# Decay attention and two gated MLPs on one core: table transfers, first weight loads, pair order of the second layer, and where each down projection begins

## The chip, the cores and the metric

The kernel runs on one core of one Trainium2 chip. The metric is the device time of one execution in microseconds (us); the lower the better. Three runs of the kernel before gave a median of 528.17 us (527.85 to 528.56).

## What is computed

Three stages follow one another, all in float32 precision (sizes: 2 batches, 8 heads, 768 positions, 64 wide; 1536 tokens of 512).

```python
# attention with decay, blocks of 64 in the reference (128 in the kernel)
out[b] = (q_b k_b^T * Dmask) v_b + (q_b * lam^(i+1)) state
state  = lam^block * state + (k_b * lam^(block-1-i))^T v_b
x = out as 1536 x 512
# first MLP
x = ((x @ w_a) * (x @ w_b)) @ w_out          # inner width 1536
# second MLP
x = max(x @ w1, x @ w2, x @ w3) @ w_out2      # inner width 768
```

## The kernel before, in words

**Precision.** TensorE multiplies float32 values as two parts each, hi and lo, and three products (hi hi, hi lo, lo hi) are added in PSUM. Every operand is therefore split first: ScalarE (ACT) copies it to hi, and VectorE (DVE) or GpSimd (POOL) subtracts to get lo. The weights come as 8-byte numbers and are converted on the core before that: one raw tile `wr` of 1 MB (768 KB for a piece of a down projection) is turned into float32 by DVE (L223, L228, L236) and ACT (L226, L232, L234). The weight tiles are numbered in one list: 0 to 11 first layer up, 12 to 19 first layer down, 20 to 28 second layer up, 29 to 32 second layer down.

**Attention.** There are 12 steps n (6 chunks of 128 positions, 2 batches). Step n needs `aq` (queries and keys) and `av` (keys and values), 512 KB each, and two decay tables made on the core: `powers` computes a row of powers per head, stores it to DRAM (`tab_d`), and `tables` (L352) and `decay_rows` (L357) read it back into the tile `tables`, in four transfers of 128 KB (the mask `dmask`) and four of 64 KB (`ltab`). In the loop over n, step n issues the loads of `aq` n+4 and `av` n+3, then the scores of n+2 (`s`, L397), their masking on DVE (`am`, L420), and the output of step n: products with the values (`o`, L436), with the state (L441), and the state's update (L448), which DVE reads (`stt`, L460, L462). The raw weight tile 0 is loaded and its conversion opened at n = 2, tile 1 at n = 7. From n = 7 on a group of plain first-layer products (`p`, L555) is put behind each step.

**Layers up.** Past the first two weight tiles of layer one, a weight tile is multiplied by one of two halves j of the tokens in seven products of a Strassen scheme (six matmuls each; L537). A tile and both halves are called a pair here. The products of neighbouring groups are interleaved by the table `SLOT`. Three PSUM banks belong to a group: `z`, `b` and `x`. Products 1, 6, 7 and 4 add into `z` one after another, and ACT copies the bank after 1, 6 and 7 (`z1`, `z6`, `z7`), so each of these copies stands between two products. In layer two the operands of half j are `y0...` and `y1...`: A11, A12, A22 and four sums S1 to S4, made by DVE and ACT from the output of the first layer down. `plan2` orders the first two pairs of layer two as (0,0), (1,0), (0,1), (1,1): tile 0 and 1 with half 0, then both with half 1.

**Layers down.** `down1` (L668) runs over k = 0 to 11 and three thirds t of the tokens: first t = 0 and 1 together, then t = 2 (`yp`, L654, 12 matmuls for each (t, k)). `down2` (L703) makes the output tiles (`out`, L700).

**What sets the order.** All queues are written by the program in one order: the class `Pace` keeps an estimate of each engine's time and puts DVE, ACT and POOL work into the stream when its gate is open. Gates are opened by hand, by `open_to("conv", item)` and `open_to("split", item)`, at points that follow TensorE's work. Each engine then works strictly in its order. All transfers of interest are issued by SyncE (SP), in one queue. Pools: 26 slots of 6 KB per partition, 5 buffers `hp` for weights and their hi and lo, 2 raw tiles, 8 PSUM banks.

Of the kernel before, what the change touches and what calls it, by code (L numbers as in the profile page):

```python
# [16 lines left out]
C = 128  # L17
# [145 lines left out]
def decay_attention_gated_mlps(ctx: ExitStack, tc: tile.TileContext, qkv: bass.AP, lam: bass.AP, wup: bass.AP, wdown: bass.AP, out: bass.AP):  # L163
# [115 lines left out]
    def down_block(m, i):  # L279
        roomy = 2 <= i < ND1 or i == ND1 + 3  # L280
# [19 lines left out]
    def items_to(m):  # L300
        while state["item"] <= min(m, len(items) - 1):
            n = state["item"]
            kind, i = items[n]
            wtask[n] = pace.opens["done", n] = pace.add((up_pair if kind == "up" else down_block)(n, i), {0: -1, 2: 0.5}.get(n, 1))
            state["item"] += 1
# [46 lines left out]
    def tables():  # L352
        for g in range(2):
            for odd in range(2):
                nc.sync.dma_start(out=dmask[:, g, odd:NP:2], in_=view((2 * odd + (g ^ odd)) * 2 * C, [[1, 128], [8 * C, NP // 2], [1, C]]))

    def decay_rows():  # L357
        for hh in range(2):
            for odd in range(2):
                nc.sync.dma_start(out=ltab[64 * hh:64 * hh + 64, odd:NP:2], in_=view((2 * odd + (hh ^ odd)) * 2 * C + C, [[0, 64], [8 * C, NP // 2], [1, C]]))  # L360
# [307 lines left out]
    def down1(at):  # L668

        ps = [[bank(f"yp{t}{e}") for e in range(KD)] for t in range(2)]  # L670
        for k in range(K1):
            for t in range(2):
                at(t, k)
                down1_part(t, k, ps[t])
        ps = [bank(f"yp2{e}") for e in range(KD)]
        for k in range(K1):
            at(2, k)
            down1_part(2, k, ps)
# [24 lines left out]
    def down2():  # L703

        n = NT // 128
        ps = [bank(f"out{i}") for i in range(6)]
        for k in range(K2):
            for i in range(6):
                down2_part(i, k, ps[i], slice(0, 512))
                if k == K2 - 1:  # L710
                    store(i, 0, 512, ps[i])
        for i in range(6, n):
            last = i == n - 1
            cols = 256 if last else 512
            for c in range(0, 512, cols):
                p = bank(f"out{i}_{c}")[:, c:c + cols]
                for k in range(K2):
                    down2_part(i, k, p, slice(c, c + cols))
                store(i, c, cols, p, last and c > 0)

    with tc.manual_schedule():
# [35 lines left out]
        def finished1(at, g):  # L757

            if g.j == 1:
# [4 lines left out]
                if m + 2 < N1:  # L764
                    open_to("split", m + 2)
                if m == K1 - 2:
# [3 lines left out]
                if m == K1 - 1:  # L770
                    for d in range(4, ND1):
# [15 lines left out]
        def layer1_steps():  # L787
# [9 lines left out]
            yield from in_slots([Group(f"u{i}_{j}", i, j, xo.get, gated) for i, j in plan], each1, finished1)  # L797

        layer1 = layer1_steps()
        for n in range(len(order)):  # L800
            load(n + 4, 0)
            load(n + 3, 1)
            if n in (2, 7):
                m = n // 4
                load_to(m)
                open_to("conv", m)
                open_to("split", m)
# [22 lines left out]
        def at1(t, k):  # L830
            if (t, k) == (2, 0):
                yo[0] = Operands([ya[0, b] for b in range(B)], "y0")
            if t == 2:
                pace.open(("y0", k - 3))
            if (t, k) == (2, 4):
                open_to("split", base + 1)
                open_to("conv", base + 2)

        down1(at1)
# [6 lines left out]
        def finished2(at, g):  # L846
            n = g.n - N1
            f, i = divmod(n, 3)
            if g.j == 1:
# [5 lines left out]
                for d in {N2 - 2: (0, 1), N2 - 1: (2, 3)}.get(n, ()):  # L855
# [15 lines left out]
        plan2 = [(0, 0), (1, 0), (0, 1), (1, 1)] + [(n, j) for n in range(2, N2) for j in range(2)]  # L871
        groups = [Group(f"v{n}{j}", N1 + n, j, yo.get, largest(n // 3, n % 3)) for n, j in plan2]
        for _ in in_slots(groups, each2, finished2):
            pass
        down2()
# [63 lines left out]
```

## Time and profile before

| what | value |
|---|---|
| median of 3 runs | 528.17 us |
| the profiled execution's own time | 528.49 us |
| its span, first to last instruction | 526.7 us |
| TensorE (PE) busy | 508.4 us, 97% |
| DVE, ACT, POOL busy | 364.1, 284.8, 50.5 us |
| PE busy in 10:50 us | 32.17 of 40 us |
| PE busy in 50:92 us | 42.00 of 42 us |
| PE busy in 230:240 us (end of layer one up) | 9.42 of 10 us |
| PE busy in 337:400 us (start of layer two up) | 60.01 of 63 us |
| PE busy in 465:480 us (end of layer two up) | 13.73 of 15 us |
| PE busy in 500:527 us (last products, last store) | 23.68 of 27 us |

Busy time is the time in which an engine has an instruction in work. A busy PE is not a PE at full clock: the table of stretches gives the granted clock too. Stretches that are not listed are without idle time on PE. Engines in the profile: PE matmul, PEld weight load, DVE VectorE, ACT ScalarE, POOL GpSimd, SP SyncE (SPq its queue).

### The profile page before, as it was taken

The page shows a single profiled execution, that of the slowest core. Times are in us where ns is not written, and L with a number is a line of the kernel's source. Part 1 is how long each engine was busy: PE and PEld are TensorE (multiplying, and loading weights), DVE is VectorE, ACT ScalarE, POOL GpSimd, SP SyncE. Part 2 cuts the span into 40 slices and gives each one's busy share as a digit, 9 for nine tenths or more (in the row PEclk, how much of TensorE's full clock was granted, in tenths as well). Part 3 has the DMA queues.
Part 4 walks back from the last instruction along what each step waited for, and adds up shares of the span by engine and source line. Part 5 has one row for each costly group of instructions (what it writes and reads, how often), then busy time and mean ns, then how long its engine had stood idle before and what let it go on. Part 6 is the DMA issues. An engine that isn't in the chain of part 4 may idle for free.

```text
span 526.7 us, 7797 instructions
## 1 busy us (share of the span) xinstructions
PE 508.4 (97%) x3175; PEld 469.2 (89%) x3175; DVE 364.1 (69%) x546; ACT 284.8 (54%) x451; POOL 50.5 (10%) x46
## 2 busy tenths in 40 slices
PE   6879999999999999999999999998999999999997
PEld 3757899999999999998888888798999999988886
DVE  3267878886677766679969268385899998689000
ACT  1257754665545555367868366445476557366211
POOL 1673000011111111111000000000000000000000
PEclk9979999999999999999999999999999999999999
DMA  7995310222222111113542200100222211020221
GB/s 225 401 403 192 103 60 0 81 80 81 80 81 82 80 44 24 54 62 120 180 160 80 81 0 22 59 1 0 81 80 82 81 60 59 2 88 33 98 83 61
DMA packets 11812, 47.96 MB, mean 91 GB/s; under 512 B 1272, under 2 KB 3072, under 8 KB 9088
## 3 DMA queue, kind: packets, MB, share of 16 engines
q1 hardware_dynamic: 11776, 47.46, 25.1%
q8 instruction: 25, 0.41, 0.3%
q14 instruction: 11, 0.09, 0.1%
HBM read 44.30 MB, written 3.15 MB: 90 GB/s over the span
## 4 chain that ended last, share of the span: by engine, by line
PE 86%; DVE 5%; DMA 4%; ACT 2%; issue 1%; SPq 1%; ACTq 0%; DVEq 0%
PE yp L654 19%; PE zu L537 16%; PE zv L537 13%; PE out L700 9%; PE bu L537 8%; PE p L555 7%; PE bv L537 7%; PE xu L537 4%; PE xv L537 3%; DMA wr<-wup_dram 2%; DMA aq<-qkv_dram 1%; PE o L436 1%; DVE m L597 1%; ACT stt L466 1%; DVE lo L187 1%
## 5 line engine op out<-in xcount | busy, mean ns | idle before, releaser
L187 DVE TENSOR_TENSOR lo<-w,hi 128x1024 fp32r<-128x1024 f32 (+1 forms) x40 | 44.1, 1109 | 11.8 <-ACT hi L190 11.8
L190 ACT ACTIVATE hi<-w 128x1024 fp32r<-128x1024 f32 (+1 forms) x40 | 37.1, 952 | 12.8 <-DVE w L187 10.1
L654 PE MATMUL yp<-gh,dh 128*128 128x512 f32 x108 | 42.0, 389 | 0.0
L654 PE MATMUL yp<-gl,dh 128*128 128x512 f32 x108 | 42.0, 389 | 0.0
L654 PE MATMUL yp<-gh,dl 128*128 128x512 f32 x108 | 42.0, 389 | 0.0
L586 POOL TENSOR_TENSOR g<-z1u,z6u 128x384 f32<-128x384 f32 x20 | 25.1, 1258 | 172.8 <-DVE z6u L568 155.4
L236 DVE TENSOR_TENSOR w<-w,ws 128x1024 f32<-128x1024 f32 x21 | 26.5, 1262 | 16.0 <-ACT w L234 15.9
L187 DVE TENSOR_TENSOR gl<-g,gh 128x512 fp32r<-128x512 f32 x36 | 25.8, 725 | 13.3 <-ACT gh L190 13.3
L228 DVE SCALAR_TENSOR_TENSOR w<-wr,w 128x1024 int32<-128x1024 int32 (+1 forms) x26 | 31.0, 1193 | 0.2
L234 ACT ACTIVATE w<-w 128x1024 f32<-128x1024 f32 (+1 forms) x26 | 26.3, 1012 | 7.4 <-DVE w L228 7.2
L226 ACT ACTIVATE ws<-wr,bias 128x1024 f32<-128x1024 f32 x21 | 25.8, 1228 | 7.6 <-DMA wr<-wup_dram 7.6
L187 DVE TENSOR_TENSOR w<-w 128x256 f32<-128x256 f32 (+1 forms) x57 | 29.0, 509 | 0.8
L190 ACT ACTIVATE z7u<-zu 128x384 f32<-128x384 f32 x20 | 9.8, 491 | 35.5 <-PE zu L537 35.4
L689 DVE COPY ob<-out 128x256 f32<-128x256 f32 x1 | 0.4, 425 | 36.9 <-PE out L700 36.9
L654 PEld LDWEIGHTS yp<-gh,dl 128*128 128x128 f32 x108 | 20.3, 188 | 4.2
L654 PEld LDWEIGHTS yp<-gl,dh 128*128 128x128 f32 x108 | 20.3, 188 | 4.2
L232 ACT ACTIVATE ws<-ws,bias 128x1024 f32<-128x1024 f32 x21 | 24.0, 1144 | 0.0
L654 PEld LDWEIGHTS yp<-gh,dh 128*128 128x128 f32 x108 | 20.3, 188 | 4.1
L223 DVE TENSOR_SCALAR w<-wr 128x1024 int32<-128x1024 int32 (+1 forms) x26 | 17.5, 674 | 8.7 <-DMA wr<-wup_dram 8.6
L190 ACT ACTIVATE ob<-out 128x512 f32<-128x512 f32 (+1 forms) x12 | 7.0, 580 | 29.2 <-PE out L700 28.8
L568 DVE TENSOR_TENSOR z7u<-bu,z7u 128x384 f32<-128x384 f32 x20 | 11.1, 556 | 15.4 <-ACT z7u L190 15.4
L190 ACT ACTIVATE gh<-g 128x512 fp32r<-128x512 f32 x36 | 21.5, 618 | 0.0
(200 smaller groups left out, 1495.2 us busy)
## 6 DMA issues: line engine op xcount, KB each, us to landing
wr<-wup_dram SPq DMA_DIRECT2D x21, 1024.0 KB, 4.8
wr<-wdown_dram SPq DMA_DIRECT2D x12, 768.0 KB, 4.3
aq<-qkv_dram SPq DMA_DIRECT2D x12, 512.0 KB, 7.3
av<-qkv_dram SPq DMA_DIRECT2D x10, 512.0 KB, 9.6
out_dram<-ob SPq DMA_DIRECT2D x11, 256.0 KB, 2.0
tables<-tab_d SPq DMA_DIRECT2D x4, 128.0 KB, 3.7
av<-qkv_dram SPq DMA_DIRECT2D x2, 256.0 KB, 4.8
tables<-tab_d SPq DMA_DIRECT2D x4, 64.0 KB, 4.1
```

The costliest lines, as they stand in the source:

```text
L187: (nc.vector if e == "DVE" else nc.gpsimd).tensor_tensor(out=o, in0=a, in1=b, op=op)
L190: nc.scalar.activation(out=o, in_=a, func=AF.Copy)
L226: nc.scalar.activation(out=sign, in_=high.bitcast(F32), func=AF.Identity, bias=bias[:, 0:1])
L228: nc.vector.scalar_tensor_tensor(out=w, in0=low, scalar=29, in1=w, op0=ALU.logical_shift_right, op1=ALU.bitwise_or)
L232: nc.scalar.activation(out=sign, in_=sign, func=AF.Sign, bias=bias[:, 1:2])
L234: nc.scalar.activation(out=f, in_=f, func=AF.Abs)
L236: nc.vector.tensor_tensor(out=f, in0=f, in1=sign, op=ALU.mult)
L537: nc.tensor.matmul(ps, w, x, start=p in FIRST and i == 0, stop=i == len(todo) - 1, skip_group_check=p not in FIRST)
L555: nc.tensor.matmul(ps, w[:, 128 * k:128 * k + 128], x[:, k], start=m == 0, stop=m == 11)
L586: nc.gpsimd.tensor_tensor(out=ga[g.n][:, tokens(g.j, 0)], in0=g.z[1], in1=g.z[6], op=ALU.mult)
L654: nc.tensor.matmul(ps[e], w[:, cols], g, start=k == 0 and m == 0, stop=k == K1 - 1 and m == 2)
L700: nc.tensor.matmul(ps, a[:, o:o + 128], w[:, s], start=k == 0 and n == 0, stop=k == K2 - 1 and n == 2)
```

## The change

- The masks come by one transfer and the decay rows by two, since the heads are now ordered on the host in the way that the tile wants them.
- Raw weight tile 0 is loaded at n = 0 and tile 1 at n = 3 (before: 2 and 7); their conversion opens at n = 3 and 6 (before: 2 and 7).
- `plan2` takes layer two pair by pair: (0,0), (0,1), (1,0), (1,1).
- `down1` and `down2` become generators. The first piece of `down1`, (t, k) = (0, 0), is issued before the last two products of layer one up; the first two pieces of `down2` (output tiles 0 and 1, k = 0) before the last two products of layer two up, one ahead of each.
- Conversions of down tiles 12, 13 and 29, 30 open a pair or so earlier; those of 18 and 19 later, inside `down1`. Down tile 13 moves to a slot, 19 to an `hp` buffer.

```diff
--- before.py
+++ after.py
@@ -277,7 +277,7 @@
     dparts, dunit = {}, {}
 
     def down_block(m, i):
-        roomy = 2 <= i < ND1 or i == ND1 + 3
+        roomy = 1 <= i < ND1 - 1 or i == ND1 + 3
         yield "gate", ("done", m - (2 if roomy or i == ND1 + 1 else 1))
         yield "gate", ("conv", m)
         t = yield from converted(m, WB, roomy)
@@ -301,7 +301,7 @@
         while state["item"] <= min(m, len(items) - 1):
             n = state["item"]
             kind, i = items[n]
-            wtask[n] = pace.opens["done", n] = pace.add((up_pair if kind == "up" else down_block)(n, i), {0: -1, 2: 0.5}.get(n, 1))
+            wtask[n] = pace.opens["done", n] = pace.add((up_pair if kind == "up" else down_block)(n, i), {0: -1, 2: 0.5, 3: 0.6}.get(n, 1))
             state["item"] += 1
 
     def open_to(what, m):
@@ -350,14 +350,11 @@
         return bass.AP(tensor=a.tensor, offset=a.offset + offset, ap=ap)
 
     def tables():
-        for g in range(2):
-            for odd in range(2):
-                nc.sync.dma_start(out=dmask[:, g, odd:NP:2], in_=view((2 * odd + (g ^ odd)) * 2 * C, [[1, 128], [8 * C, NP // 2], [1, C]]))
+        nc.sync.dma_start(out=dmask.rearrange("p g a i -> p (g a) i"), in_=view(0, [[1, 128], [2 * C, H], [1, C]]))
 
     def decay_rows():
         for hh in range(2):
-            for odd in range(2):
-                nc.sync.dma_start(out=ltab[64 * hh:64 * hh + 64, odd:NP:2], in_=view((2 * odd + (hh ^ odd)) * 2 * C + C, [[0, 64], [8 * C, NP // 2], [1, C]]))
+            nc.sync.dma_start(out=ltab[64 * hh:64 * hh + 64], in_=view(hh * NP * 2 * C + C, [[0, 64], [2 * C, NP], [1, C]]))
 
 
     order = [(b, c) for c in range(NC) for b in range(B)]
@@ -667,11 +664,14 @@
 
     def down1(at):
 
-        ps = [[bank(f"yp{t}{e}") for e in range(KD)] for t in range(2)]
+        ps = {}
         for k in range(K1):
             for t in range(2):
+                if k == 0:
+                    ps[t] = [bank(f"yp{t}{e}") for e in range(KD)]
                 at(t, k)
                 down1_part(t, k, ps[t])
+                yield
         ps = [bank(f"yp2{e}") for e in range(KD)]
         for k in range(K1):
             at(2, k)
@@ -703,12 +703,15 @@
     def down2():
 
         n = NT // 128
-        ps = [bank(f"out{i}") for i in range(6)]
+        ps = {}
         for k in range(K2):
             for i in range(6):
+                if k == 0:
+                    ps[i] = bank(f"out{i}")
                 down2_part(i, k, ps[i], slice(0, 512))
                 if k == K2 - 1:
                     store(i, 0, 512, ps[i])
+                yield
         for i in range(6, n):
             last = i == n - 1
             cols = 256 if last else 512
@@ -763,12 +766,15 @@
                         open_to("conv", d)
                 if m + 2 < N1:
                     open_to("split", m + 2)
+                if m == K1 - 3:
+                    for d in range(2):
+                        open_to("conv", N1 + d)
                 if m == K1 - 2:
                     for d in range(2):
                         open_to("conv", N1 + d)
                         open_to("split", N1 + d)
                 if m == K1 - 1:
-                    for d in range(4, ND1):
+                    for d in range(4, 6):
                         open_to("conv", N1 + d)
                         open_to("split", N1 + d)
                     for d in range(2):
@@ -794,17 +800,35 @@
                         pace.open(("x1", "sums"))
                     if j == 1:
                         finished1(0, Group("", i, j, None, None))
-            yield from in_slots([Group(f"u{i}_{j}", i, j, xo.get, gated) for i, j in plan], each1, finished1)
-
+            groups = [Group(f"u{i}_{j}", i, j, xo.get, gated) for i, j in plan]
+            for i, _ in enumerate(in_slots(groups, each1, finished1)):
+                if 7 * len(groups) - i == 3:
+                    next(then)
+                yield
+
+        def at1(t, k):
+            if t == 0 and k in (5, 8):
+                open_to("conv", N1 + (k + 7) // 2)
+                open_to("split", N1 + (k + 7) // 2)
+            if (t, k) == (2, 0):
+                yo[0] = Operands([ya[0, b] for b in range(B)], "y0")
+            if t == 2:
+                pace.open(("y0", k - 3))
+            if (t, k) == (2, 4):
+                open_to("split", base + 1)
+                open_to("conv", base + 2)
+
+        yo = {}
+        then = down1(at1)
         layer1 = layer1_steps()
         for n in range(len(order)):
             load(n + 4, 0)
             load(n + 3, 1)
-            if n in (2, 7):
-                m = n // 4
-                load_to(m)
-                open_to("conv", m)
-                open_to("split", m)
+            if n in (0, 3):
+                load_to(n // 3)
+            if n in (3, 6):
+                open_to("conv", n // 3 - 1)
+                open_to("split", n // 3 - 1)
             if n == 9:
                 load_to(NPLAIN + 1)
                 open_to("conv", NPLAIN)
@@ -827,16 +851,8 @@
         for _ in layer1:
             pass
 
-        def at1(t, k):
-            if (t, k) == (2, 0):
-                yo[0] = Operands([ya[0, b] for b in range(B)], "y0")
-            if t == 2:
-                pace.open(("y0", k - 3))
-            if (t, k) == (2, 4):
-                open_to("split", base + 1)
-                open_to("conv", base + 2)
-
-        down1(at1)
+        for _ in then:
+            pass
         for i in range(7):
             pace.open(("y0", i))
             pace.open(("y1", i))
@@ -852,7 +868,7 @@
                         open_to("conv", base + d)
                 if n + 2 < N2:
                     open_to("split", base + n + 2)
-                for d in {N2 - 2: (0, 1), N2 - 1: (2, 3)}.get(n, ()):
+                for d in {N2 - 3: (0,), N2 - 2: (1,), N2 - 1: (2, 3)}.get(n, ()):
                     open_to("conv", base + N2 + d)
                     open_to("split", base + N2 + d)
             if i == 2:
@@ -868,11 +884,14 @@
                 for k in (f, f + K2 // 2):
                     ha[k] = slot(f"m{k}")
 
-        plan2 = [(0, 0), (1, 0), (0, 1), (1, 1)] + [(n, j) for n in range(2, N2) for j in range(2)]
+        plan2 = [(n, j) for n in range(N2) for j in range(2)]
         groups = [Group(f"v{n}{j}", N1 + n, j, yo.get, largest(n // 3, n % 3)) for n, j in plan2]
-        for _ in in_slots(groups, each2, finished2):
+        then = down2()
+        for i, _ in enumerate(in_slots(groups, each2, finished2)):
+            if 7 * len(groups) - i in (3, 2):
+                next(then)
+        for _ in then:
             pass
-        down2()
 
 
 def kernel(**inputs):
@@ -928,7 +947,7 @@
     wup = np.ascontiguousarray(np.concatenate([
         blocks(ua[:, 0], ub[:, 0], ua[:, 1], ub[:, 1]), np.stack(third, axis=1).reshape(-1, 128, 1024)])).view(np.int64)
     wdown = np.ascontiguousarray(np.concatenate([down(wo), down(wm)])).view(np.int64)
-    arrays = {"qkv": qkv, "lam": np.asarray(inputs["lam"]).reshape(H, 1), "wup": wup, "wdown": wdown}
+    arrays = {"qkv": qkv, "lam": np.asarray(inputs["lam"])[[2 * a + (g ^ a % 2) for g in range(2) for a in range(NP)]].reshape(H, 1), "wup": wup, "wdown": wdown}
     nc = bacc.Bacc("TRN2", target_bir_lowering=False, num_devices=1, dynamic_dma_scratch_size=2048)
     args = [nc.dram_tensor(n + "_dram", a.shape, mybir.dt.from_np(a.dtype), kind="ExternalInput").ap() for n, a in arrays.items()]
     args.append(nc.dram_tensor("out_dram", (NT, DM), F32, kind="ExternalOutput").ap())
```

The order of instructions that results is shown at three places. Numbers behind names count tiles of the program.

DVE in the attention, steps n = 1 to 4, before (`am4` is the masking of step 4, `stt` the state, `w0` the conversion of weight tile 0):

```order
L460 COPY stt_81<-o1_1_241 128x256
L223 TENSOR_SCALAR w0_282<-wr0_270 128x1024
L420 TENSOR_TENSOR am4_288<-s4_0_272,tables_79 128x512
L420 TENSOR_TENSOR am4_288<-s4_1_273,tables_79 128x512
L228 SCALAR_TENSOR_TENSOR w0_282<-wr0_270,w0_282 128x1024
L462 TENSOR_TENSOR stt_81<-o2_1_292,stt_81 128x256
L420 TENSOR_TENSOR am5_342<-s5_0_329,tables_79 128x512
```

and in the change:

```order
L457 COPY stt_81<-o1_1_238 128x256
L417 TENSOR_TENSOR am4_279<-s4_0_267,tables_79 128x512
L417 TENSOR_TENSOR am4_279<-s4_1_268,tables_79 128x512
L459 TENSOR_TENSOR stt_81<-o2_1_283,stt_81 128x256
L223 TENSOR_SCALAR w0_331<-wr0_175 128x1024
L228 SCALAR_TENSOR_TENSOR w0_331<-wr0_175,w0_331 128x1024
L417 TENSOR_TENSOR am5_338<-s5_0_321,tables_79 128x512
```

The first instruction that reads the raw tile stood ahead of the masking of step 4; it now stands behind that masking and behind the state of step 2.

ACT at the start of layer two up, before (`y10`, `y11` hold half 1 of the output of `down1`, `z1v00`, `z6v00`, `z7v00` copies of the first group's bank):

```order
L190 ACTIVATE z1v00_3106<-zv00_3096 128x384
L190 ACTIVATE y1A11_3103<-y10_2850 128x768
L190 ACTIVATE y1A12_3104<-y10_2850 128x768
L190 ACTIVATE y1A22_3105<-y11_3074 128x768
L190 ACTIVATE y1S1_3118<-y1s12_3093 128x768
L190 ACTIVATE z6v00_3130<-zv00_3096 128x384
L190 ACTIVATE y1S2_3129<-y1s12_3093 128x768
L190 ACTIVATE z7v00_3150<-zv00_3096 128x384
```

and in the change:

```order
L190 ACTIVATE z1v00_3095<-zv00_3085 128x384
L190 ACTIVATE y1A11_3092<-y10_2828 128x768
L190 ACTIVATE y1S1_3106<-y1s12_3082 128x768
L190 ACTIVATE y1S2_3108<-y1s12_3082 128x768
L190 ACTIVATE y1A12_3093<-y10_2828 128x768
L190 ACTIVATE z6v00_3120<-zv00_3085 128x384
L190 ACTIVATE y1A22_3094<-y11_3058 128x768
L190 ACTIVATE y1S3_3140<-y11_3058 128x768
L190 ACTIVATE z7v00_3143<-zv00_3085 128x384
```

The order of the operand copies changed, and the copy of S3 moved ahead of `z7v00`.

ACT just ahead of that, in the copies of the last results of `down1` (`yp21` to `yp23`), before:

```order
L190 ACTIVATE y10_2850<-yp21_2868 128x128
L190 ACTIVATE y11_3074<-yp21_2868 128x384
L190 ACTIVATE y10_2850<-yp22_2869 128x128
L190 ACTIVATE y11_3074<-yp22_2869 128x384
L190 ACTIVATE y10_2850<-yp23_2870 128x128
```

and in the change:

```order
L190 ACTIVATE y10_2828<-yp21_2846 128x128
L190 ACTIVATE y11_3058<-yp21_2846 128x384
L226 ACTIVATE ws22_3070<-wr22_2751,bias_75 128x1024
L190 ACTIVATE y10_2828<-yp22_2847 128x128
L190 ACTIVATE y11_3058<-yp22_2847 128x384
L190 ACTIVATE y10_2828<-yp23_2848 128x128
```

An instruction of the conversion of weight tile 22 (L226) came in between these copies.

## Rows read from the trace of the kernel before

**Rows 1.** The page's first line.

```profile
span 526.7 us, 7797 instructions
```

**Rows 2.** Who waited for whom, PE, whole span: us in total, times, longest us.

```profile
PE s L397 <- DVE am L420: 3.5, 1, 3.5
...
PE o L436 <- DVE am L420: 2.1, 2, 1.1
PE bv L537 <- DVE lo L187: 1.7, 1, 1.7
...
PE zv L537 <- ACT z6v L190: 1.3, 1, 1.3
...
PE zv L537 <- ACT z7v L190: 0.7, 1, 0.7
PE zu L537 <- ACT z7u L190: 0.6, 1, 0.6
PE bv L537 <- DVE z7v L568: 0.5, 1, 0.5
```

**Rows 3.** Timeline of the attention: start us, us, engine, line, operation, idle before.

```profile
10.02 0.69 DVE L420 TENSOR_TENSOR am<-s,tables 128x512 f32<-128x512 f32 x1 [5.59 <-DMA tables<-tab_d]
...
11.42 1.89 DVE L420 TENSOR_TENSOR am<-s,tables 128x512 f32<-128x512 f32 x3 [0.72 <-DMA tables<-tab_d]
...
20.52 1.16 PE L397 MATMUL s<-aq 64*128 64x128 f32 x16 [0.66 <-DMA aq<-qkv_dram]
...
23.84 1.16 PE L397 MATMUL s<-aq 64*128 64x128 f32 x16
...
26.58 1.06 POOL L410 TENSOR_TENSOR av<-av,tables 128x512 f32<-128x512 f32 x1 [0.16 <-DMA av<-qkv_dram]
...
29.39 0.70 DVE L223 TENSOR_SCALAR w<-wr 128x1024 int32<-128x1024 int32 x1 [8.64 <-DMA wr<-wup_dram]
...
30.74 2.33 PE L397 MATMUL s<-aq 64*128 64x128 f32 x16 [3.50 <-DVE am L420]
...
36.59 1.16 PE L397 MATMUL s<-aq 64*128 64x128 f32 x16
```

**Rows 4.** Chain of work that ended last, 0:70: start us, us, what.

```profile
17.18 12.19 DMA wr<-wup_dram
...
48.15 2.51 PE p L555 x12
```

**Rows 5.** Stretches: busy us (instructions) by engine, granted clock, DMA share, GB/s.

```profile
12.00:13.00 1.00, 0.83 (x8) 0.83 (x10) 1.00 (x3) 0.00 (x0) 0.53 (x1) 0.54 1.33 242
...
15.00:16.00 1.00, 1.00 (x14) 1.00 (x16) 0.42 (x1) 0.46 (x2) 0.20 (x1) 0.75 0.94 360
...
30.00:32.00 2.00, 1.26 (x10) 1.26 (x11) 2.00 (x4) 1.22 (x3) 0.11 (x1) 0.50 1.02 420
```

**Rows 6.** The page's DMA issues: KB each, median us from issue to landing.

```profile
tables<-tab_d SPq DMA_DIRECT2D x4, 128.0 KB, 3.7
...
tables<-tab_d SPq DMA_DIRECT2D x4, 64.0 KB, 4.1
```

**Rows 7.** The chain again, end of layer one up and down: start us, us, what.

```profile
234.02 1.04 PE xu L537 x6
...
236.69 1.33 PE zu L537 x6
...
239.23 97.96 PE yp L654 x432
```

**Rows 8.** The chain again, start of layer two up.

```profile
338.78 0.74 ACT y1A L190
...
340.51 0.88 DVE y1s L187
...
342.26 0.39 ACT z6v L190
```

**Rows 9.** The page's costliest groups: busy us, mean ns of one | idle before.

```profile
L226 ACT ACTIVATE ws<-wr,bias 128x1024 f32<-128x1024 f32 x21 | 25.8, 1228 | 7.6 <-DMA wr<-wup_dram 7.6
```

## The prediction, made before the result was known

> **What bounds the kernel now.** I read the page's head first: the span is 526.7 us [rows 1], and PE is busy in nearly all of it, so only two things can move the time: PE's idle stretches and PE at half clock. The change removes no matmul. So the second view is the list of PE's waits over the whole span [rows 2]: its seven rows that the change can touch add up to 10.4 us. Third, the timeline of the attention [rows 3], to see what stands behind the two largest. At 27.2 us PE has finished step 3 and waits 3.5 us for a masking on DVE. DVE itself had stood still for 8.64 us, but not for data of the attention: ahead of that masking in its order is the first instruction on raw weight tile 0, and the chain shows why it waits: the tile was issued at 17.18 and took 12.19 us to land, behind the loads ahead of it in the queue [rows 4]. That is the first thing to see: a weight that nobody needs yet blocks the engine that feeds PE. The second is in the stretches [rows 5]: behind this wait the granted clock is 0.50, the lower of the two levels, 1.2 GHz. The scores at 30.74 take 2.33 us where those at 20.52 take 1.16, and from there to the next scores at 36.59 are 5.85 us, where a whole step at full clock takes 3.32 (20.52 to 23.84) [rows 3]. So the wait of 3.5 costs 2.5 more. From 48.15 on, when the plain products begin [rows 4], PE is dense until 236.
>
> **Front, what it becomes.** SP's order up to the load of `av` 3 keeps its sequence, with eight table transfers turned into three. The bytes are the same, and the four mask transfers already overlap: 3.7 us each to land [rows 6], yet the last half is there at 11.42, 1.4 us after the first [rows 3]. The new single transfer is therefore worth little in itself. I let it land at 11.2, between 10.0 and 11.4, the two halves' times now; the first masking is then later by 1.2 us and the second a little earlier. Fewer issues close gaps on the DMA queue: I take 0.7 us for everything behind (bounds 0 and 1.5). PE's scores of step 4, which now wait for their load until 20.52, then start at 19.8.
>
> Next is what is moved past what. At 420 GB/s [rows 5], a load of 512 KB takes 1.25 us; raw tile 0 took from about 26.5, where the load of `av` 5 landed and released POOL, to 29.37, so 2.5 to 2.9 us [rows 3]. It now stands ahead of `aq` 5, `av` 4, `aq` 6 and `av` 5, which stood ahead of it. It lands at 19.8 + 1.25 + 2.5 = 23.5, just when DVE reaches its conversion, which is now behind the masking of step 4 and behind the state of step 2. So the 8.64 us on DVE and the 3.5 on PE go. What is late instead is `aq` 5: 19.8 + 2.5 (two loads) + 2.5 (the tile) = 24.8, while PE, at 3.32 a step, wants it at 23.1. That is a new wait of 1.7 us. Later loads keep up: 28.1 is when PE wants `aq` 6, and it is there at 27.3; raw tile 1, now ahead of `aq` 8, puts that load at 24.8 + 8 x 1.25 = 34.8, and PE wants it at 24.8 + 3 x 3.32 = 34.8. DVE, which loses 8.64 us of standing still, keeps up with this.
>
> Does the new wait bring the half clock? The nearest rows: waits of 1.1 and 1.0 close together (the two of 2.1 in sum) [rows 2] were followed by 0.54 in 12:13 and 0.75 in 15:16, some 3.4 us at half [rows 5]; the wait of 0.66 at 20.52 [rows 3] by none. 1.7 is nearer the former, so I take such a stretch: 3.4 us at half is 1.7 us of work lost. Then the plain products start at 19.8 + 6 x 3.32 + 1.7 + 1.7 = 43.1 instead of 48.15: **5.0 us gained** (without half clock 6.7; with the stretch as long as that behind the present wait, and 1 us of other waits, 2.5). Everything between here and 236 is released by PE's own results and loads that come earlier, so I let the shift carry through.
>
> One rule weighs on this. By the Trainium skill, "DMA: Bandwidth & Descriptors", section "Anatomy of one DMA", a transfer costs about 2.0 us fixed plus its bytes at 436 GB/s (fitted for the GpSimd path; here SP issues); by that a single mask transfer takes an estimated 3.2 us, lands at 9.0, and the front is 2.2 us better than mine, total 519.3. The trace speaks against it: the small transfers' latencies run side by side.
>
> **End of layer one up.** Now PE waits 0.6 us for the copy `z7u` [rows 2] and the product behind starts slowly (1.33 instead of 1.04) [rows 7]. In the change the first piece of `down1`, 12 matmuls of 97.96/432 = 0.227, 2.7 us, stands between product 7 and product 4, and the copy is long done. It needs the splits of the first gate tile and down tiles 12 and 13, which DVE now has earlier. Gain **0.9**. Next tight: bank `yp11`, which waits for the last group's product on DVE, behind four conversion rows there; my count leaves PE and DVE equal, so 0 to 0.5 is lost.
>
> **Start of layer two up.** Two waits of now, 1.3 (`z6v`) and 1.7 (`lo`) [rows 2]. The second goes: tile 22's hi and lo wait for the two `hp` buffers of tile 20, whose last product was the 26th of the layer and becomes the 19th, with the third pair starting at the 29th in both. But half 1's operands are now needed 7 products after `down1` ends, not 14, and they can't be begun earlier. Count from the end of `down1`. ACT: the last copy of results ends at 0.7 now; the L226 row among them (1.2 [rows 9]) makes it 1.8. Then `z1v` (0.4), four operand copies of 0.75, `z6v` (0.4) [rows 8]: 5.6. PE has done its four free products at 4.4: 1.3 of waiting, with 0.2 before at `z1v`. DVE: from 1.8 two sums, four subtractions, one addition, the third sum, 7 x 0.88 + 0.5 [rows 8]: 8.5; ACT's copy of S3 waits for it, `z7v` stands behind that, to 9.7; PE, having done products 7, 1 and 5 by 8.8, waits 0.9 for it. Two more of 0.4 and 0.5 follow, where `z1v` and `z6v` of half 1 stand behind conversion rows on ACT. In sum 3.3 against 1.3 + 1.7 = 3.0: **0.3 lost**. Bounds: gain 1.7 (only the first wait stays) to loss 5 (all of y1, 14 us of DVE and ACT in turn, ahead of half 1's first product at 6).
>
> **End of layer two up.** Waits of 0.7 and 0.5 [rows 2], for the copy `z7v` and the addition behind it. One output piece of 3 x 0.227 = 0.7 us ahead of each covers 0.7 and 0.5; the copy and addition before are no later. Gain **1.1**. The end (last copy and store) stays.
>
> **Sum.** 5.0 + 0.9 - 0.3 + 1.1 = 6.7 us. The profiled execution took 528.49 for its span of 526.7, 0.3 above the median of 528.17; it becomes 521.8, and the median **521.5**.
>
> **Rivals.**
> - *No half clock.* The wait of 0.66 [rows 3] passed without it; the new one may be shorter if the DMA gaps close further. 519.8, or 518.5 with the queue 1.5 us earlier. Chance 0.2; the page's rule above, 519.3, falls in here and gets 0.05 more.
> - *Half 1 is late.* Copies on ACT wait for sums on DVE, and PE's banks wait for ACT: each estimate of mine could be short. With the whole of y1 ahead of its first product the loss is 5 instead of 0.3: 526.2; half of that, 524. Chance 0.13.
> - *The change doesn't do it at the front.* If the raw tile lands later than DVE gets to it by as much as PE's slack, or several attention loads are late by it, a wait is only swapped: the plain products start at 46 or later, 524.5 or more. For: the DMA queue has no spare time (share 1.02 in 30:32 [rows 5]); against: the bytes ahead of tile 0 shrink by four loads. Chance 0.06.
> - *Slower: one table transfer goes at one transfer's pace.* Place: the first masking, for which everything waits. If the four in flight at once are what makes them quick, 1024 pieces of 512 bytes take 4 x 3.7 us, landing at 20.6: the front's gain is gone, 526.5. At the pace of the 64 KB transfers (128 pieces in 4.1 us) they take 33 us and land at 38.6: 544. It decides at a landing of about 23.4, from which the kernel is slower by 0.2%. Against it: while the tables pass the DMA engines are already busy (share 1.33 in 12:13 [rows 5]), so more in flight adds nothing. Chance 0.03.
>
> **How the numbers follow.** Forecast 0.53, no half clock 0.25, half 1 late 0.13, front swapped 0.06, slow transfer 0.03. The likeliest gives 521.5. Below go 518.8 (no half clock and the earlier queue), above 525 (most of the late half 1); about 2 in 10 lie outside. A measurement here tells about 0.2%, 1.1 us, from no change: faster means below 527.1. Forecast, no half clock, most of late half 1 and of the swapped front lie there: 0.93. Same 0.03, slower 0.04, most of it the slow transfer.
>
> **What would show it.** Right: DVE's wait for `wr` on L223 gone, PE's 3.5 us wait replaced by one for `aq` at 23 to 25 us, the first `p` product near 43 (41.4 at full clock), no wait for `z7u` before `yp`, no `lo` wait in layer two but waits for `z6v` and `z7v` of 3 us in sum just behind `down1`, none for `z7v` at the end. Wrong: a first masking past 14 us; a `p` product after 46; more than 5 us of waits behind `down1`; new waits of `yp` on weights.

## The result, and the profile after

The change takes **520.55 us** (median of 4 runs, 520.47 to 520.75); the kernel before took 528.01 in the same comparison (527.39 to 528.56). The ratio is 0.9856, 95% interval 0.9843 to 0.9870: 7.5 us faster, where 6.7 were forecast. The profiled execution took 520.75 us. Its page begins:

```profile
span 519.0 us, 7790 instructions
```

The span is 7.7 us shorter than [rows 1]. PE's waits over the whole span (us in total, times, longest us):

```profile
PE o L433 <- DVE am L417: 3.9, 1, 3.9
...
PE zv L534 <- ACT z6v L190: 1.2, 1, 1.2
PE s L394 <- DMA aq<-qkv_dram: 1.0, 1, 1.0
PE zv L534 <- ACT z7v L190: 1.0, 2, 0.7
PE p L552 <- DVE x0A L187: 0.4, 1, 0.4
```

Against [rows 2], the 3.5 us for a masking behind the raw tile, the `lo` wait of 1.7, `z7u` and the addition behind `z7v` are gone. `z6v` stayed. The wait for the first masking grew from 2.1 to 3.9, and one for a load of `aq` is new. The timeline of the attention (start us, us, engine, line, operation, idle before):

```profile
12.62 2.48 DVE L417 TENSOR_TENSOR am<-s,tables 128x512 f32<-128x512 f32 x4 [8.39 <-DMA tables<-tab_d]
...
13.36 2.36 PE L433 MATMUL o<-am,av 128*64 128x128 f32 x15 [3.86 <-DVE am L417]
...
21.06 1.16 PE L394 MATMUL s<-aq 64*128 64x128 f32 x16
...
25.27 0.68 DVE L223 TENSOR_SCALAR w<-wr 128x1024 int32<-128x1024 int32 x1
...
25.43 1.16 PE L394 MATMUL s<-aq 64*128 64x128 f32 x16 [0.98 <-DMA aq<-qkv_dram]
...
42.08 0.62 PE L552 MATMUL p<-x0A,hi 128*128 128x384 f32 x2
```

L223 has no idle time in front of it, where [rows 3] has 8.64 us. The first `p` is at 42.08 instead of 48.15. The granted clock by stretch (columns as in [rows 5]):

```profile
12.00:13.00 1.00, 0.00 (x0) 0.00 (x0) 0.39 (x1) 0.00 (x0) 0.34 (x1) 0.50 1.12 322
15.00:16.00 1.00, 1.00 (x16) 1.00 (x13) 0.10 (x1) 0.38 (x1) 0.00 (x0) 0.50 1.05 430
18.00:19.00 1.00, 1.00 (x16) 1.00 (x16) 0.20 (x1) 0.78 (x4) 0.82 (x2) 0.71 1.05 430
24.00:26.00 2.00, 1.02 (x26) 0.91 (x24) 1.04 (x3) 1.26 (x5) 0.00 (x0) 1.00 1.03 422
```

Half clock (1.2 GHz) lies around and behind the wait for the table, up to 18 to 19 us; the wait for `aq` has none. From 15 us on the DMA engines move 422 to 430 GB/s (322 in 12:13). The page's DMA issues (KB each, median us to landing), beside [rows 6]:

```profile
tables<-tab_d SPq DMA_DIRECT2D x1, 512.0 KB, 6.8
...
tables<-tab_d SPq DMA_DIRECT2D x2, 128.0 KB, 8.3
```

The chain at the end of layer one up, beside [rows 7]: the piece of `down1` stands between `xu`'s `zu` and the last `zu`, which takes 1.06 instead of 1.33, with no gap.

```profile
229.52 1.04 PE zu L534 x6
230.56 2.76 PE yp L651 x12
233.32 1.06 PE zu L534 x6
```

The timeline at the start of layer two up, beside [rows 8]:

```profile
329.90 1.21 ACT L226 ACTIVATE ws<-wr,bias 128x1024 f32<-128x1024 f32 x1
331.00 1.21 ACT L190 ACTIVATE y<-yp 128x128 f32<-128x128 f32 x4
...
335.71 0.47 ACT L190 ACTIVATE z6v<-zv 128x384 f32<-128x384 f32 x1
...
336.23 0.62 PE L534 MATMUL zv<-y0S,hi 128*128 128x384 f32 x2 [1.24 <-ACT z6v L190]
...
339.04 0.84 ACT L190 ACTIVATE y1S<-y 128x768 fp32r<-128x768 f32 x1 [2.12 <-DVE y L187]
...
340.31 0.61 PE L534 MATMUL zv<-y0A,hi 128*128 128x384 f32 x2 [0.68 <-ACT z7v L190]
```

PE's marks in the two traces (us):

| | before | after | gained in the stage |
|---|---|---|---|
| first product of layer one up (`zu`) | 92.42 | 86.88 | 5.54 |
| end of layer one up | 239.23 | 235.43, with 2.76 of `down1` done | 1.02 |
| first `zv` | 337.03 | 330.51 | -0.04 |
| end of layer two up | 474.45 | 467.47, with two pieces of `down2` done | 1.82 with the end of `down2` |
| last PE work | 523.68 | 515.34 | |
| end of span | 526.7 | 519.0 | -0.60 |

They sum to 7.7, as the span. The last row goes with the merged tables: from PE's last work to the end of the span it is 3.03 us in the kernel before and 3.04 in run 3, the two with eight table transfers, and 3.62 to 3.64 in the twelve traces with three. The last store lands equally late behind PE in both (2.18 and 2.19 us). Behind it, SP has four more closing waits to run in the change (0.2 us), which the kernel before runs ahead of the landing, and POOL pauses 0.3 us longer among its closing instructions; why the merge brings this isn't shown.

### The profile page after: what moved, and what is told of

Same layout as the page of the kernel before. It is cut to its first block, busy times and chain, and to the rows that moved or that the text cites. A ratio compares the mean times of both kernels' runs of the same rounds, so it can differ in the third digit from the quotient of the medians.

```text
span 519.0 us, 7790 instructions
## 1 busy us (share of the span) xinstructions
PE 505.3 (97%) x3175; PEld 467.8 (90%) x3175; DVE 365.4 (70%) x546; ACT 285.0 (55%) x451; POOL 51.7 (10%) x46
## 4 chain that ended last, share of the span: by engine, by line
PE 85%; DMA 6%; DVE 4%; ACT 2%; SPq 1%; issue 0%
PE yp L651 18%; PE zu L534 16%; PE zv L534 12%; PE out L700 9%; PE bu L534 8%; PE p L552 6%; PE bv L534 6%; PE xu L534 4%; DMA av<-qkv_dram 4%; PE xv L534 3%; DMA aq<-qkv_dram 2%; PE o L433 1%; DVE m L594 1%; DVE y1S L187 1%; ACT y1S L190 0%; ACT y L190 0%
## 5 line engine op out<-in xcount | busy, mean ns | idle before, releaser
L226 ACT ACTIVATE ws<-wr,bias 128x1024 f32<-128x1024 f32 x21 | 25.8, 1230 | 0.0
L417 DVE TENSOR_TENSOR am<-s,tables 128x512 f32<-128x512 f32 x24 | 15.2, 681 | 9.8 <-DMA tables<-tab_d 8.4
L534 PE MATMUL zu<-x1A,hi 128*128 128x384 f32 x80 | 20.3, 334 | 0.0
```

What stands on the lines that cost most here:

```text
L226: nc.scalar.activation(out=sign, in_=high.bitcast(F32), func=AF.Identity, bias=bias[:, 0:1])
L534: nc.tensor.matmul(ps, w, x, start=p in FIRST and i == 0, stop=i == len(todo) - 1, skip_group_check=p not in FIRST)
```

## The experiments

The theory (A): nearly all of the gain comes from the place of the first weight loads, which no longer block DVE; the attention is now bound by the stream of loads; each of the three smaller parts gives about what its PE waits were. Rivals: the merged tables give part of it, the conversion's place in DVE's order and not the load's gives it, the half clock matters, the pair order costs what its half 1 waits cost. All edits are to the changed kernel; ratios are to the kernel before on the same chip. Runs 2, 6 and 8 (and the one with the edits of runs 5 and 8 together) were on another chip than the rest, so their distance to the others is surer by the ratios.

**The change again**, beside the runs that follow: 520.50 us (519.15 to 523.27), ratio 0.9854 (0.9831 to 0.9878). First `p` at 42.80, waits 2.3 for the first masking and 3.0 for `aq`.

**1. First loads back at their old places.**

```diff
-            if n in (0, 3):
-                load_to(n // 3)
-            if n in (3, 6):
-                open_to("conv", n // 3 - 1)
-                open_to("split", n // 3 - 1)
+            if n in (2, 7):
+                m = n // 4
+                load_to(m)
+                open_to("conv", m)
+                open_to("split", m)
```

> The changed kernel with the loads and conversions of raw weight tiles 0 and 1 put back to steps 2 and 7; the merged tables and all later parts stay. Theory A (the front's gain comes from the weight tile's place alone): DVE stands still for 8 us or more on the first weight row again, PE waits 3 us or more for a masking, the plain products start near 48 us, and the time is 525.5 to 526.5. Theory B (the tables give part of the front's gain): the plain products start at 46 or earlier and the time is 523 to 524.5.

Measured: 527.42 us (526.79 to 529.30), ratio 0.9977 (0.9965 to 0.9990). DVE's timeline in it:

```profile
28.38 0.69 DVE L223 TENSOR_SCALAR w<-wr 128x1024 int32<-128x1024 int32 x1 [7.22 <-DMA wr<-wup_dram]
```

PE's waits in it:

```profile
PE s L394 <- DVE am L417: 2.8, 1, 2.8
...
PE zu L534 <- ACT z6u L190: 0.9, 2, 0.6
```

DVE stands still again, PE waits behind it, and the first `p` is at 47.2. So the places of loads and conversions together are worth 6.9 us, most of the gain, and more than theory A expected (525.5 to 526.5). Not all of that lies in the attention: 4.6 by the first `zu` (91.47 against 86.88), and 1.4 in layer one up, where waits for `z6u` appear that neither kernel has.

**2. Early load, old place of the conversion.** Only the second half of edit 1: the tiles land early, but L223 stands ahead of the masking of step 4 again.

```diff
-            if n in (3, 6):
-                open_to("conv", n // 3 - 1)
-                open_to("split", n // 3 - 1)
+            if n in (2, 7):
+                open_to("conv", n // 4)
+                open_to("split", n // 4)
```

> Raw tiles 0 and 1 are loaded at n = 0 and 3 as in the change, but their conversion is opened at n = 2 and 7 as before, so the first instruction on the raw tile stands ahead of the masking of step 4 again. Theory A (what cost the time was the landing of the tile, since its place in DVE's order only matters while the tile is under way): DVE reaches it near 20 and waits for it to about 22 to 23.5, PE waits 0 to 1.5 us for that masking, median 520.5 to 522.5. Theory B (the place in DVE's order is what counts): PE waits 3 us or more for the masking of step 4, half clock behind it, median 524 to 527.

Measured: 523.14 us (521.25 to 524.35), ratio 0.9900 (0.9883 to 0.9918). Timeline:

```profile
23.51 0.69 DVE L223 TENSOR_SCALAR w<-wr 128x1024 int32<-128x1024 int32 x1 [2.66 <-DMA wr<-wup_dram]
...
24.84 1.16 PE L394 MATMUL s<-aq 64*128 64x128 f32 x16 [1.56 <-ACT ws L226]
...
41.66 0.59 PE L552 MATMUL p<-x0A,hi 128*128 128x384 f32 x2
```

Between the two expectations. By the medians the earlier load alone gives 4.3 of the 6.9 us (527.42 to 523.14; 4.1 by the ratios), and the later conversion the other 2.6 (2.4). The trace shows the first part, but not the second at the masking: DVE stands still for 2.66 us, and PE doesn't wait for that masking at all. The wait of 1.56 is for `aq` 5, which lands at 24.71, 0.13 us ahead of the scores; that is the distance in the change too (25.30 and 25.43), and the L226 that the profile names ends at about the same time. The profiled execution is the fastest of the four (521.25), and its attention is no slower than the change's. What it loses is in layer one up: waits of 0.8 for `z6u`, and 1.4 in that stage in all. The place of the other executions' further 2 us wasn't seen.

**3. Eight table transfers again**, in the old head order; the edit is the table part of the diff, undone.

> The changed kernel with the old eight table transfers (and the old order of heads in the decay vector). Theory A (the scores of step 5 wait for their load, so whatever comes earlier is covered): the first masking starts near 10.0 instead of 12.6 us, PE's wait for the load of queries 5 grows from 1.0 to about 2 us or stays, and the time stays within 0.8 us of 520.55. Rival C (the late single transfer and the 6.8 us of half clock behind it cost what PE loses there): the time falls by 1.5 to 3 us, to 517.5 to 519.

Measured: 520.28 us (519.44 to 520.72), ratio 0.9839 (0.9824 to 0.9855). The first masking is at 10.32 instead of 12.62, PE waits only 0.8 us for it, and then longer for the loads behind:

```profile
PE s L397 <- DMA aq<-qkv_dram: 2.6, 1, 2.6
```

The first `p` is at 43.2. Merging the tables gives nothing at the front: whatever PE gains at the table it waits for `aq`. At the end of the span it costs the 0.6 us above, which the medians are too coarse to show.

**4. The clock held up** while PE waits for the table, by 16 more warming matmuls.

```diff
-        keep_warm(8)
+        keep_warm(24)
```

> The changed kernel with 24 instead of 8 dummy matmuls behind the first scores, which keep PE busy until near 12.8 us. Theory A: the half clock between 11.7 and 18.6 us goes or shortens, the scores of step 4 start near 20 instead of 21.06, but those of step 5 still wait for their load to 25.4, and the time stays within 0.4 us of 520.55. Rival C (the half clock there sets the front): 518.5 to 519.5.

Measured: 520.60 us (519.88 to 520.84), ratio 0.9845 (0.9830 to 0.9859). Two of its stretches:

```profile
18.00:19.00 1.00, 1.00 (x19) 0.88 (x19) 0.52 (x2) 0.04 (x1) 0.86 (x2) 1.00 1.03 414
24.00:26.00 2.00, 0.88 (x15) 0.91 (x16) 1.77 (x3) 1.51 (x6) 0.00 (x0) 1.00 1.05 426
```

PE's timeline, step 5:

```profile
25.12 1.16 PE L394 MATMUL s<-aq 64*128 64x128 f32 x16 [1.40 <-ACT stt L463]
```

Full clock at 18:19, where the change has 0.71, and yet the scores of step 5 start at 25.12 against 25.43. The half clock at the start costs nothing: the load of step 5 sets the time. The profile names `stt` on ACT for this wait; the trace has `aq` 5 landing at 24.98, 0.14 us ahead of the scores as in the change.

**5. Raw tile 0 loaded one step later** (`load_to(0)` at n = 1).

```diff
-            if n in (0, 3):
+            if n in (1, 3):
```

> The changed kernel with raw weight tile 0 loaded at step 1 instead of step 0, so that the queries of step 5 and the values of step 4 are loaded ahead of it. Theory A (the tile ahead of queries 5 causes PE's wait of 1.0 us): that wait goes, DVE waits some 1.3 us on the first weight row without holding PE up, and the time is about 519.6. Rival D (PE's wait only moves to the next load, or to DVE): the time stays at 520.3 to 520.8.

Measured: 519.90 us (519.17 to 520.22), ratio 0.9832 (0.9818 to 0.9847). Between the two expectations. PE waits 3.2 us in 3 for `aq`, and 0.6 more in one that the profile puts down to an L226; there too an `aq` had landed 0.13 us before. The edit moves the wait among loads; 0.6 below the change is inside the intervals.

**6. Table and `aq` 2 in another order**: the decay rows are issued ahead of `load(2, 0)`.

```diff
         tables()
-        load(2, 0)
         decay_rows()
+        load(2, 0)
```

> The load of aq 2 is issued behind the two transfers of decay rows instead of ahead of them, so that the mask transfer has only smaller company at first. Theory A (the single mask transfer, 5.69 to 12.5, goes at a pace of its own: 1024 pieces of 512 bytes): it still lands at 12 to 12.6, the first masking stays at 12 to 12.7. Theory B (it lands late because the 512 KB of aq 2 take the DMA engines beside it): it lands at 10.5 to 11.5 and the first masking comes 1 us or more sooner. The time changes little in both, 519.5 to 521, since the loads behind bound the front.

Measured: 519.91 us (519.40 to 520.54), ratio 0.9832 (0.9818 to 0.9847). The page's DMA issues:

```profile
tables<-tab_d SPq DMA_DIRECT2D x1, 512.0 KB, 5.6
...
tables<-tab_d SPq DMA_DIRECT2D x2, 128.0 KB, 5.6
```

PE's timeline from the scores of step 5:

```profile
24.35 1.16 PE L394 MATMUL s<-aq 64*128 64x128 f32 x16 [1.90 <-ACT stt L463]
25.44 1.81 PE L433 MATMUL o<-am,av 128*64 128x128 f32 x16
```

The first masking is at 11.58, within B's reach, but the order of the change gave 9.88 to 12.62 too (below), so this settles nothing about the cause. The time says once more that the table isn't the bound: the wait of 1.90 is again for `aq` 5 (landing at 24.22), with half clock behind it.

**7. The old order of the first pairs of layer two.**

```diff
-        plan2 = [(n, j) for n in range(N2) for j in range(2)]
+        plan2 = [(0, 0), (1, 0), (0, 1), (1, 1)] + [(n, j) for n in range(2, N2) for j in range(2)]
```

> The changed kernel with the old order of the first two pairs of layer two, all else as in the change. Theory A (pair by pair swaps a wait of 1.7 us for a lo of tile 22 and one of 1.3 for two of 1.2 and 0.7 us): those old waits are back, the two new ones are gone or one stays, and the time is 1.0 to 1.2 us above the change. Rival E (pair by pair costs about what it gives, as forecast): within 0.4 us of the change, or below it.

Measured: 522.00 us (521.37 to 522.66), ratio 0.9879 (0.9862 to 0.9895): 1.5 more than the change. PE's waits:

```profile
PE bv L534 <- DVE lo L187: 1.7, 1, 1.7
PE zv L534 <- ACT z6v L190: 1.2, 1, 1.2
PE zv L534 <- ACT z7v L190: 0.7, 1, 0.7
```

The `lo` wait is back at its old size; `z6v` doesn't change. The pair order takes away the one and costs nearly nothing. The intervals of the two ratios overlap, so the verdict rests on the trace: from the first `zv` to PE's last work it has 186.7 us, the change 184.8.

**8. Tile 22 converted later**, to keep its L226 row from between the copies of `y` on ACT.

```diff
                 open_to("split", base + 1)
-                open_to("conv", base + 2)
```

> The conversion of tile 22, opened inside down1 in the change, opens when the pair of tile 20 ends, so that no L226 row stands between the last copies of down1's results on ACT, and no L223 and L228 rows ahead of the sums of y1 on DVE. Theory A (the waits for z6v and z7v behind down1 come from these conversion rows, 1.2 us on ACT): the z6v wait of 1.2 us goes or falls below 0.4, z7v's first falls too, and the median is 519 to 519.6. Rival (the sums of y1 are the chain, whatever stands ahead): the waits stay within 0.3 us. Rival (tile 22 becomes late): a wait for lo of tile 22 of 1 us or more 25 to 30 us behind down1's end, median 520.5 or above.

Measured: 523.49 us (522.11 to 524.23), ratio 0.9896 (0.9876 to 0.9917). Timeline behind `down1`:

```profile
333.36 0.84 ACT L190 ACTIVATE y1S<-y1s 128x768 fp32r<-128x768 f32 x1 [1.16 <-DVE y1s L187]
334.11 0.47 ACT L190 ACTIVATE z6v<-zv 128x384 f32<-128x384 f32 x1
...
334.64 0.62 PE L534 MATMUL zv<-y0S,hi 128*128 128x384 f32 x2 [1.31 <-ACT z6v L190]
...
361.02 0.44 PE L534 MATMUL zv<-y0A,lo 128*128 128x384 f32 x1 [2.88 <-DVE lo L187]
```

The stretch behind the last of these waits:

```profile
362.00:365.00 3.00, 3.00 (x11) 3.00 (x11) 1.79 (x2) 2.93 (x4) 0.00 (x0) 0.50 0.16 25
```

Theory A falls for `z6v`: without the row on ACT the same wait stays, since a copy of a sum now stands ahead of `z6v` and waits 1.16 us for DVE. The `z7v` waits went, as expected. In their place tile 22 is late by 2.88 us, with half clock behind it. The edits of runs 5 and 8 together:

> The edit of tile 22 together with raw tile 0 loaded one step later (n = 1), which alone gave 519.9. If the two gains lie in different places and add up: 518.4 to 519.3, the first p near 42, waits behind down1 below 1 us. If the later tile 22 only moves the wait: 519.7 to 520.3.

Measured: 522.62 us (522.04 to 523.94), ratio 0.9887 (0.9869 to 0.9904), with the same `lo` wait of 2.9. No better version was found.

**9. No piece of `down1` within layer one up.** `down1` starts when layer one up has ended.

```diff
-                if 7 * len(groups) - i == 3:
-                    next(then)
```

> The changed kernel without the first piece of the first layer down ahead of the last two products of layer one up. Theory A: the wait of 0.6 us for the copy z7u is back, and the time is 0.8 to 1.1 us above the change. Rival (the wait was already gone by the earlier front): within 0.3 us.

Measured: 521.16 us (520.33 to 521.64), ratio 0.9861 (0.9845 to 0.9877), 0.7 more than the change. The wait of 0.6 returns as in [rows 2], and one of 0.2 behind it:

```profile
PE zu L534 <- ACT z7u L190: 0.6, 1, 0.6
PE bu L534 <- DVE z7u L565: 0.2, 1, 0.2
```

**10. No pieces of `down2` within layer two up.**

```diff
-            if 7 * len(groups) - i in (3, 2):
-                next(then)
+            pass
```

> The changed kernel without the two first output pieces between the last products of layer two up. Theory A: waits of 0.7 and 0.5 us for z7v are back, and the time is 0.8 to 1.2 us above the change. Rival (the conversions that were moved earlier had already removed them): within 0.3 us.

Measured: 521.20 us (521.11 to 521.75), ratio 0.9866 (0.9851 to 0.9881), 0.7 more. PE's waits:

```profile
PE s L394 <- DMA aq<-qkv_dram: 3.9, 3, 1.5
...
PE zv L534 <- ACT z7v L190: 1.7, 2, 1.0
...
PE bv L534 <- DVE z7v L565: 0.8, 1, 0.8
PE o L433 <- DVE am L417: 0.6, 2, 0.4
```

Two waits at the end of layer two up, of 1.0 for `z7v` and 0.8 for the addition behind it, are back (the other 0.7 for `z7v` is at its start). In this execution the table landed early (4.1 us after its issue, first masking at 9.88), and its waits show the exchange: 0.6 for the masking, 3.9 for `aq`. The loads behind the table came early too: `aq` 5 landed at 23.68 (25.30 in the change), the scores of step 5 start at 23.82, and the first `p` at 40.46, 1.6 us sooner than in the change. This early front hides most of what the edit costs. The two waits at the end are longer than the 0.7 and 0.5 of [rows 2], and half clock follows them here, which it does in neither kernel:

```profile
464.00:467.00 3.00, 3.00 (x9) 2.81 (x10) 1.65 (x4) 0.84 (x1) 0.00 (x0) 0.50 0.00 0
```

For runs 9 and 10 each median's excess of 0.7 is no larger than the spread of the change's own runs; the traces carry the verdict.

**The stages in the traces.** The front differs between executions with the landing of the loads: the first `p` is at 40.46 to 42.80 in the six traces with the front of the change (the change, its second execution, runs 7 to 10). The stages behind it agree to 0.1 us in all runs whose edit leaves them alone, so they show prices that the medians can't (us):

| | change | before | run 1 | run 2 | run 7 | run 8 | run 9 | run 10 |
|---|---|---|---|---|---|---|---|---|
| first `zu` to first `zv` | 243.63 | 244.61 | 245.10 | 245.07 | 243.63 | 243.66 | 244.91 | 243.65 |
| first `zv` to PE's last work | 184.82 | 186.66 | 184.81 | 184.83 | 186.71 | 187.73 | 184.83 | 187.66 |

The pair order is worth 1.9 us here, the piece of `down1` 1.3, the pieces of `down2` 2.8. With the 6.9 of run 1 that is more than the 7.5 of the whole change: runs 1 and 10 bring waits, and run 10 half clock, that the kernel before doesn't have. So each number is what the part is worth within the change, and not its share of the gain.

## Why the prediction was right, and where it wasn't

The time was 1.0 us below the forecast of 521.5 and inside the range. By its steps:

- **What blocks PE.** Right. The raw tile ahead of a masking on DVE was the cause, and runs 1 and 2 show that its late landing made it so. That the place in DVE's order counts as well is shown by run 2's time alone; its trace has no wait for that masking.
- **Front, 5.0 forecast, 5.5 measured** to the first `zu`. What sets it was right: the load of `aq` 5, and five steps of 3.32 behind it. 25.43 + 5 x 3.32 = 42.0 is the first `p`, measured 42.08; the forecast was 24.8 + 1.7 + 5 x 3.32 = 43.1. The load released PE 0.6 later than forecast, the 1.7 of half clock did not come, and of the 6.1 gained at the first `p` 0.5 was lost by the first `zu`, 0.4 of it in a wait for `x0A` that was not foreseen. That 5.5 lies so near 5.0 is in part luck. The table was to land at 11.2, at most 11.4: the first masking came at 12.62, and the scores of step 4 at 21.06 instead of 19.8. This cost nothing more, since it only shortened the wait for `aq` 5 from the forecast 1.7 to 0.98.
- **The table's transfer.** "Worth little in itself" was right at the front, by run 3. The traces of the single transfer have 4.1 to 6.8 us from issue to landing, and the rival of a slow one (landing at 20.6 or later) falls by them. By the Trainium skill, "DMA: Bandwidth & Descriptors", section "Anatomy of one DMA", whose figures are fitted for transfers that GpSimd issues, it would take an estimated 3.2. SP issues this one, the traces don't agree, and the measurement decides.
- **Half clock.** This step failed: the nearest row was chosen wrongly. The forecast put 1.7 us of waiting beside two waits of 1.1 and 1.0. But [rows 2] also has a single wait of 1.7, for `lo` in layer two up, and the clock behind it (at 369.01) stayed at 1.00 in the kernel before (the line below). The wait that came, 0.98, brought none, nor did waits of 1.40 to 1.56 us before step 5 in the change's second execution and runs 2, 3, 4, 7, 8, 9 and 10. In run 6 the wait of 1.90 did (the products with the values took 1.81 instead of 1.09), and in run 10 the two of 1.0 and 0.8 at the end. The rival "no half clock" came true at that place; its 519.8 didn't, with the load 0.6 later, 0.5 lost behind the first `p` and 0.6 at the end of the span, against which layer two up and its `down2` gained 1.0 more than forecast.

```profile
369.00:372.00 3.00, 2.99 (x17) 3.00 (x18) 2.46 (x3) 1.03 (x1) 0.00 (x0) 1.00 0.11 14
```

- **End of layer one up, 0.9 forecast, 1.0 measured** in the trace; run 9's price is 0.7 by time and 1.3 by its trace. The piece lasted 2.76 against 2.7, and no wait on bank `yp11` came.
- **Start of layer two up, 0.3 lost forecast, 1.1 gained** by the waits (0.8 by the marks, with the end's 1.0 taken off the 1.82). This step failed. The waits were to sum to 3.3 against 3.0; they are 1.24 + 0.68 = 1.92. These two were nearly sized right (1.3 and 0.9); the 0.2 at `z1v` and the two of 0.4 and 0.5 for half 1 did not occur. Run 7 puts the pair order at 1.5 us by time and 1.9 by the trace, near the 1.7 of the wait that it removes. The reason given for 1.3 (the L226 row) wasn't the only one: run 8, without that row on ACT, has the same wait behind a sum on DVE.
- **End of layer two up, 1.1 forecast, 1.0 measured** in waits (1.27 to 0.29; the last 0.29 for `z7v` was not foreseen). Run 10's price is 0.7 by time and 2.8 by its trace.
- **The end** was to stay. It became 0.6 longer, in every trace with the merged tables.

## What to carry to other kernels

When PE waits for an engine that is itself idle, read what stands first in that engine's queue: here an instruction on data that nobody needed yet held up the masking. Loading that data earlier gave most of it; putting its consumer later gave time too, but the trace doesn't show where. Once this block was gone, the next bound was the stream of loads, and then neither a sooner table nor a higher clock ahead of the late load was worth anything. A piece of the next stage put between two dependent products hid a copy at no cost, as its operands were there. Here the front differed by 2.3 us between executions of one order, so the length of a stage in the traces told more of the small parts than the medians did.

## What the runs showed of the hardware

- One and the same table transfer of 512 KB took 4.1 to 6.8 us from issue to landing from one execution to the next, and the first masking came between 9.88 and 12.62, with the order in the queue up to it unchanged. Four transfers of 128 KB took 3.7 [rows 6] and 3.9.
- The first `p` follows the landing of `aq` 5, and not the masking. With the masking 2.3 us sooner (run 3) that load lands later (26.42 against 25.30) and the first `p` is at 43.20; with 2.7 sooner (run 10) it lands at 23.68, and the first `p` is at 40.46. Each is 16.8 us behind the landing, as in the change. With 1.0 sooner (run 6) it lands at 24.22, and the half clock behind the wait takes that back. In the stretches shown from 15 to 26 us the DMA engines are full (share 1.03 to 1.05, 414 to 430 GB/s).
- Conversions that open at another place in the attention changed waits far behind it: the `z6u` waits of 0.8 to 0.9 us in layer one up (in run 2 the longest ends at 98.2 us) appear only in runs 1 and 2, and the stage is 1.4 us longer there. Why wasn't tried.
